# An attention, mixing and FFN kernel: weights in one lasting place per chunk, the first pairs' working memory laid where the later pairs' will be, pooled attention of a later pair ranked ahead, sums in place

## The chip, the cores and the metric

The kernel runs on one core of a Trainium2 chip. Its time is the device time in microseconds (us) of one execution. Times of one kernel differ a little from run to run: the three runs of the kernel before took 1030.01, 1033.21 and 1035.8 us. What is predicted is the median of such runs of the changed kernel.

## The reference

Two heads of a batch are handled together and are called a *pair* here: 8 batches of 8 heads make 32 pairs, four to a batch.

```
q_d, k_d, v_d = means of q, k, v over 4 neighbouring positions      # 576 -> 144
out_up    = repeat(softmax(q_d k_d^T / 8) v_d, 4)                    # pooled attention
out_local = softmax(q k^T / 8 where |i-j| < 4, else -1e9) v          # 7 neighbours
x  = (out_up + out_local), heads side by side                        # [8, 576, 512]
h  = x^T U V        (U: 576 x 32, V: 32 x 576)                       # mixing over positions
u  = x + h^T
out = u + relu(u w_ch1) w_ch2       (512 -> 2048 -> 512, the FFN)
```

## The kernel before, in words

**Precision.** TensorE works on numbers of a shorter format. So every operand of the large products is split into a high part and a low part (`W1H`/`W1L`, `uH`/`uL`, `hH`/`hL`), and one product becomes three matmuls: high by high, high by low, low by high.

**The FFN** is cut into steps (batch, t, fc): 8 batches, two halves t of 288 positions, 16 chunks fc of 128 hidden columns, 256 steps in all. `ffn1` (L889) makes one chunk of the hidden layer with 12 matmuls into a PSUM bank `ps_h`; ScalarE (ACT) writes `hH` (L897), VectorE (DVE) writes `hL` (L898); `ffn2` (L913) adds the chunk to four accumulators `acc` with 12 matmuls. Step i of `ffn2` stands about three steps behind step i of `ffn1`. The first 19 steps of `ffn1` have only one bank, `h0`, so each waits for the `hL` of the one before it; after that the banks h0 and h1 alternate.

**The weights.** Each of 16 chunks of w_ch1 and 16 of w_ch2 (512 KB each) is loaded raw and converted by `convert`: an ACT operation (L343), three DVE operations (L345, L347, L349), an ACT operation for the high part (L354) and a GpSimd (POOL) operation for the low part (L357). The DVE operations use a PSUM bank `y`: an accumulator's (`acc2`/`acc3`) for w_ch1, the bank h1 for w_ch2. The raw chunks of w_ch1, and the first three of w_ch2, share three buffers with `Pt`, a tile of the later pairs, so a load waits until a buffer comes free. The converted w_ch1 lies in two large tiles that last; the converted w_ch2 lies in `w2p`, a region that the pool `early` holds until the first batch's attention has ended. The operation called "late" hands it over. The first `ffn2` also waits for all 16 high parts of w_ch1, because their conversion uses its accumulators' banks.

**The attention** has two forms. The four pairs of batch 0 (*early pairs*) are done on the chip in one go (`early_global`, `local_blocks`, `early_mix`), with working tiles in the pool `early`. The other 28 (*late pairs*) go through memory:

- `late_global`: loads `gq` and `gT` (L580), POOL averages them (L429, L431), `late_scores` makes local and pooled scores in one bank (`ps_b`, L720 and L727), and the local scores are stored as `s_s`; then exponentials `E`, their transposes `ps_t`, the product `ps_a`, the scaled result `od` (L567), stored four-fold as `up_s` (L572).
- `local_attn`: the local scores come back as `sc`; a chain of small DVE and ACT operations (`ms` L771, `lmx`, `lsm`, `lrl`) ends in the weights `at`; `up_s` comes back as `ul`; five times, ACT copies a piece of `ul` into `Pt`, POOL multiplies seven shifted values into it (L800) and DVE sums it into `acc` (L805, an SBUF tile of this function, not the accumulator); `acc` is stored as `x_s`.
- `mix_part`: `x_s` is loaded twice, as `xL` and as `Y`; DVE transposes Y (L839), POOL makes the low part of xL (L841), TensorE (PE) makes `ps_hu` (L849) and `ps_u` (L864), and the result is split into `uH` (ACT) and `uL` (POOL, L872) for the FFN.

**The order of the work** is set when the program is built. A planner plays through all operations with estimated durations and, on each engine, takes among those that are ready the one with the smallest priority number. The pairs count 0, 10, 20 and so on (a pair's scores a little earlier, its local part +1, its mixing +2), weights have numbers of their own, the FFN's matmuls 1000 and more, so that they fill what is left. What comes out is one fixed order for each engine. On the chip each engine follows its order and waits where it must. All transfers are issued by SP, in its fixed order too.

Of the kernel before, what the change touches and what calls it, by code (L numbers as in the profile page):

```python
# [51 lines left out]
class Plan:  # L52
# [9 lines left out]
    def op(self, eng, dur, fn, r=(), w=(), prio=0.0, after=(), lat=None, move=0.0, at=0.0):  # L62
# [137 lines left out]
def attn_mix_ffn_kernel(ctx: ExitStack, tc, q, kp, vp, qT, kT, v, U, Ub, V, w1, w2, mask, band, eye, ex, pool, vw, vn, ident, outT):  # L200
# [16 lines left out]
    W1S, W2P, W2S = 2, 20, 1  # L217
# [5 lines left out]
    W1P = 20  # L223
    W2D = 4
# [68 lines left out]
    w2p = Late()  # L293
# [36 lines left out]
    dma(lambda: nc.sync.dma_start(out=mask_sb, in_=mask), [], ["mask"], 35, 32)  # L330

    def convert(raw, pp, n, hi_out, lo_out, a, wkey, name, prio, gate=(), l0=0):
        t = buf(ffn, [128, CN], I32, name, "cT:" + name, 3)
        if gate or name == "cu" and lo_out is not None:
# [17 lines left out]
        if gate:  # L352
            done.append(plan.ops[-1])
        act(n, lambda: nc.scalar.activation(hi_out(), ta(), AF.Copy), [t, *gate], own("H"), prio)  # L354
# [6 lines left out]
    def early_raw(name):  # L361
        return buf(early_pool, [128, S], I32, name, "eraw", 1)

    def raw_buf(name):
# [676 lines left out]
```

## Time and profile before

| what | value |
|---|---|
| median of three runs | 1033.21 us |
| the profiled execution | 1031.25 us, its span from the first to the last instruction 1029.4 us |
| mean granted TensorE clock | 0.983 |
| PE busy over the span | 990.8 us (96%) |
| DVE, ACT, POOL busy | 504.4, 390.2, 550.6 us |
| first FFN matmul (batch 0) | starts at 77.15 us |
| first `ffn2` matmul | starts at 91.34 us |
| first FFN matmul of batch 1 | starts at 219.88 us |

"Busy" is the time in which an engine had at least one instruction under way. Rows with `[x <-E y]` say that the engine stood idle for x us before the row, and that what ended it was engine E's work on y. "x12" is a count of like instructions. The 1.85 us by which the profiled execution is longer than its span lie around the program.

### The profile page before, as it was taken

The numbers are of one execution on the slowest core, as the hardware profiler recorded it, in microseconds if no ns is written. First come the engines' busy times: TensorE is split into PE (matmuls) and PEld (weight loads), VectorE is DVE, ScalarE is ACT, GpSimd is POOL, SyncE is SP. The second block draws the span as 40 slices with busy tenths as digits, with TensorE's granted clock in tenths as the row PEclk, the third lists the DMA queues.
The fourth block names the chain that finished last, engine by engine and source line by source line (L and its number), as shares of the span: only waits on it lengthen the run. The fifth ranks groups of instructions, "written<-read, shape, count | busy, mean of one in ns | idle before, by whom it ended". The sixth has DMA issues, their size and how long they took to land.

```text
span 1029.4 us, 26839 instructions
## 1 busy us (share of the span) xinstructions
PE 990.8 (96%) x10792; PEld 972.9 (95%) x10792; DVE 504.4 (49%) x1022; ACT 390.2 (38%) x1239; POOL 550.6 (53%) x580
## 2 busy tenths in 40 slices
PE   5888979989999999999999999999999999999998
PEld 4677979989999999999999999999999999999998
DVE  4778986544454447544454545445654424212111
ACT  3667643433334334443343442334443232111110
POOL 3545895783756656685665756457575605211010
PEclk8899999989999999999999999999999999999999
DMA  9748854573454546555544453556555231000000
GB/s 291 200 136 237 256 132 123 133 154 98 103 142 105 142 118 148 121 120 144 121 126 115 122 122 83 122 134 156 126 135 129 78 76 35 24 1 24 1 24 24
DMA packets 222452, 120.51 MB, mean 117 GB/s; under 512 B 174756, under 2 KB 198136, under 8 KB 222328
## 3 DMA queue, kind: packets, MB, share of 16 engines
q1 hardware_dynamic: 222328, 118.79, 46.0%
q8 instruction: 85, 1.39, 0.6%
q14 instruction: 39, 0.32, 0.1%
HBM read 87.89 MB, written 30.86 MB: 115 GB/s over the span
## 4 chain that ended last, share of the span: by engine, by line
PE 90%; DVE 3%; ACT 2%; DMA 2%; issue 1%; SPq 1%; POOL 0%; DVEq 0%; ACTq 0%
PE acc L913 38%; PE ps_h L889 38%; PE ps_a L563 3%; PE ps_b L720 2%; PE ps_hu L849 2%; PE ps_t L550 1%; PE ps_b L727 1%; PE ps_u L864 1%; PE ps_v L445 1%; DMA w2r<-in_W 1%; DVE ms L771 1%; DMA ul<-up_s 1%; PE ps_u L695 1%; DMA pool_sb<-in_pool 0%; PE ps_hu L675 0%
## 5 line engine op out<-in xcount | busy, mean ns | idle before, releaser
L913 PE MATMUL acc<-hH,W 128*128 128x288 f32 x2048 | 464.0, 299 | 0.1
L913 PEld LDWEIGHTS acc<-hH,W 128*128 128x128 f32 x2048 | 344.8, 188 | 1.6 <-POOL W L357 0.5
L889 PE MATMUL ps_h<-uH,W1H 128*128 128x288 f32 x1024 | 305.9, 299 | 11.1 <-DVE hL L898 11.1
L889 PE MATMUL ps_h<-uL,W1H 128*128 128x288 f32 x1024 | 304.2, 297 | 0.0
L898 DVE SCALAR_TENSOR_TENSOR hL<-ps_h,hH 128x288 fp32r<-128x288 f32 x256 | 116.7, 456 | 382.4 <-ACT hH L897 381.6
L889 PE MATMUL ps_h<-uH,W1L 128*128 128x288 f32 x1024 | 302.9, 296 | 0.0
L913 PE MATMUL acc<-hL,W 128*128 128x288 f32 x1024 | 301.9, 295 | 0.0
L800 POOL TENSOR_TENSOR Pt<-vl,at 128x896 f32<-128x896 f32 (+1 forms) x140 | 241.9, 1806 | 90.3 <-DVE acc L805 40.2
L897 ACT ACTIVATE hH<-ps_h 128x288 fp32r<-128x288 f32 x256 | 105.1, 411 | 432.1 <-PE ps_h L889 431.8
L889 PEld LDWEIGHTS ps_h<-uH,W1H 128*128 128x128 f32 x1024 | 194.3, 190 | 12.9 <-DVE hL L898 12.6
L889 PEld LDWEIGHTS ps_h<-uH,W1L 128*128 128x128 f32 x1024 | 194.7, 190 | 0.0
L889 PEld LDWEIGHTS ps_h<-uL,W1H 128*128 128x128 f32 x1024 | 194.4, 190 | 0.0
L913 PEld LDWEIGHTS acc<-hL,W 128*128 128x128 f32 x1024 | 192.7, 188 | 0.0
L805 DVE TENSOR_REDUCE acc<-Pt 128x128 f32<-128x1024 f32 (+1 forms) x140 | 151.1, 1105 | 6.7 <-ACT Pt L794 2.4
L841 POOL TENSOR_TENSOR xL<-xL,xH 116x640 fp32r<-116x640 f32 x28 | 44.0, 1572 | 96.5 <-ACT xH L840 83.5
L872 POOL TENSOR_TENSOR uL<-xT,uH 128x288 fp32r<-128x288 f32 x56 | 44.3, 816 | 84.5 <-ACT uH L870 84.4
L924 POOL TENSOR_TENSOR o<-uH,uL 128x288 f32<-128x288 f32 x64 | 49.8, 817 | 53.0 <-DMA out_t<-o 53.0
L521 POOL TENSOR_TENSOR vr<-vr 72x256 f32<-72x256 f32 x56 | 41.6, 743 | 41.7 <-DMA vr<-in_v 37.0
L745 ACT ACTIVATE se<-ps_b 96x114 f32<-96x114 f32 x112 | 40.0, 357 | 59.3 <-PE ps_b L720 37.8
L794 ACT ACTIVATE Pt<-ul 128x128 f32<-128x128 f32 (+1 forms) x140 | 50.3, 444 | 18.7 <-DVE acc L805 14.5
L536 ACT ACTIVATE E<-ps_b,nb 72x144 f32<-72x144 f32 x112 | 40.9, 372 | 0.6
L531 DVE TENSOR_REDUCE mx<-ps_b 72x2 f32<-72x288 f32 x56 | 23.4, 449 | 27.6 <-ACT se L745 27.6
(137 smaller groups left out, 986.4 us busy)
## 6 DMA issues: line engine op xcount, KB each, us to landing
vl<-in_vp SPq DMA_DIRECT2D x56, 240.0 KB
out_t<-o SPq DMA_DIRECT2D x64, 144.0 KB
w1r<-in_W SPq DMA_DIRECT2D x16, 512.0 KB
w2r<-in_W SPq DMA_DIRECT2D x16, 512.0 KB
gT<-in_kT SPq DMA_DIRECT2D x28, 291.0 KB
gq<-in_qT SPq DMA_DIRECT2D x28, 288.0 KB
vr<-in_v SPq DMA_DIRECT2D x56, 144.0 KB
up_s<-od SPq DMA_DIRECT2D x112, 72.0 KB
```

The source lines that it names most:

```text
L521: pool_tt(256, lambda x=x: nc.gpsimd.tensor_tensor(out=x()[:, :, 0:2, :], in0=x()[:, :, 0:2, :], in1=x()[:, :, 2:4, :], op=ALU.add), [x], ...
L536: act(SD, lambda a=a, hh=hh, nb=nb: nc.scalar.activation(Es[hh]()[:, a, :], pooled_view(ps[hh])[:, a], AF.Exp, bias=nb()[:, a:a + 1], scal ...
L794: act(n * D, lambda n=n, ps=ps, Pt=Pt: nc.scalar.activation(Pt()[:, :n, :, 7], ul()[:, ps, :], AF.Copy), [ul], [(Pt, 1)], prio, 0.16)
L800: nc.gpsimd.tensor_tensor(out=Pt()[:, :n, :, 0:7].rearrange("p s d o -> p o s d"), in0=win, in1=at()[:, ps, :].rearrange("p s o -> p o s") ...
L805: dve(8.5 * n * D, lambda n=n, ps=ps, Pt=Pt: nc.vector.tensor_reduce(out=acc()[:, ps, :], in_=Pt()[:, :n], axis=AX.X, op=ALU.add), [(Pt, 0 ...
L841: pool_tt(640, lambda: nc.gpsimd.tensor_tensor(out=xL(), in0=xL().bitcast(F32), in1=xH().bitcast(F32), op=ALU.subtract), [xL, xH], [xL], prio)
L872: pool_tt(TN, lambda uH=uH, uL=uL, uf=uf: nc.gpsimd.tensor_tensor(out=uL()[:, hp, :], in0=uf(), in1=uH()[:, hp, :].bitcast(F32), op=ALU.su ...
L889: nc.tensor.matmul(ps()[:, :TN], w[:, dc, fs], u()[:, dc, :], start=(n == 0), stop=(n == 3 * NDC - 1))
L897: last_h[i] = act(TN, lambda: nc.scalar.activation(hH(), ps()[:, :TN], AF.Relu), [ps], [hH], FIRST, 0.05)
L898: dve(TN, lambda: nc.vector.scalar_tensor_tensor(hL(), ps()[:, :TN], 0.0, hH().bitcast(F32), op0=ALU.max, op1=ALU.subtract), [ps, hH], [hL ...
L913: nc.tensor.matmul(ac[e]()[:, :TN], W2[fc]()[:, w, es], hx(), start=(fc == 0 and n == 0), stop=(fc == NFC - 1 and n == 2))
L924: pool_tt(TN, lambda e=e, o1=o1: nc.gpsimd.tensor_tensor(out=o1()[:, :TN], in0=uH()[:, e, :].bitcast(F32), in1=uL()[:, e, :].bitcast(F32), ...
```

## The change

**Weights.** Every chunk, of w_ch1 and of w_ch2, now has one lasting place in a pool `wts`, opened first. The raw chunk lands there and the converted one, of the same size, takes its place. A load waits for the conversion four chunks back (`WD`). The chunks come in a new sequence: the first four of w_ch1, then one of w_ch1 and one of w_ch2 in turn, with priority numbers from 30 up (before, w_ch1 had 20 to 50, and w_ch2 20 to 35 behind "late"). The first 12 chunks are converted through the accumulators' banks and the first `ffn2` waits for their high parts alone; the other 20 go through the bank h1. U's blocks and V, needed by the early pairs, land raw in places of the last w_ch2 chunks.

**Memory.** The pool `early` now lies where the late pairs' pools `loc`, `glo` and `mix` will be. These open when the first batch's attention has ended ("late"), and every operation on their tiles comes after that. The FFN no longer waits for "late".

**Ranks.** `late_global` of a pair gets the number p - 10.5 in place of p: ahead of the local part of the pair before it.

**Sums in place.** `Pt` is summed back into `ul` (two buffers now); the tile `acc` goes. `gh`, the first average, and `od` share one buffer in the late pairs. The early pairs' `ps_hu` and `ps_u` use the accumulators' banks 0 and 1.

The instructions are the same in number and kind: 8792 matmuls, 1024 DVE, 1113 ACT, 585 POOL and 884 SP instructions in both, as the order lists them.

The core of the diff:

```diff
+        deps.update(d for k in (*r, *w) for d in getattr(getattr(k[0] if isinstance(k, tuple) else k, "pool", None), "gate", ()))
...
-    W1S, W2P, W2S = 2, 20, 1
+    W1F, WS = 4, 0.4
-    W1P = 20
-    W2D = 4
+    W1P = 30
+    WD = 4
+    LEAD = 10.5
+    NA = 12
...
-        if gate or name == "cu" and lo_out is not None:
+        if own_bank:
             y = buf(ps_h, [128, CN], I32, "y_h", "h1:" + name, 1)
...
-    def raw_buf(name):
-        return buf(loc, [128, 2 * CN], I32, name, "Pt:raw", 3)
+    def raw_in(f, name):
+        return buf(wts, [128, 2 * CN], I32, name, f"W2_{f}:{name}")
...
+    W1 = [buf(wts, [128, 2, NDC, 128], F32R, f"W1_{f}", f"W1_{f}:w") for f in range(NFC)]
+    W2 = [buf(wts, [128, 2, DM], F32R, f"W2_{f}", f"W2_{f}:w") for f in range(NFC)]
+    weights, done = [], []
+
+    def load_w(w, src, hi, lo, a, prio, dprio):
+        weights.append(w)
+        raw = buf(wts, [128, 2 * CN], I32, "wr", w.tag + ":raw")
+        dma(lambda: nc.sync.dma_start(out=raw(), in_=src), [], [raw], dprio, 525,
+            after=done[len(done) - WD:len(done) - WD + 1] if len(done) >= WD else ())
+        convert(raw, 128, CN, hi, lo, a, w, "c" + w.tag[1], prio, len(done) >= NA)
...
-        gh = work(e, glo, [128, SD, 2], F32, "gh")
+        gh = work(e, glo, [128, SD, 2], F32, "gh", None if e else "god:h")
-        od = g([QH, 4, D], "od")
+        od = buf(glo, [QH, 4, D], F32, "od", "god:o", 1)
-        ph = psum(ps_m, "ps_hu", "m:x", 2)
+        ph = psum(ps_acc, "ps_hu", "acc0:x", 1)
-            pu = psum(ps_m, "ps_u", "m:x", 2)
+            pu = psum(ps_acc, "ps_u", f"acc{1 - t}:x", 1)
-        acc = lb([128, NPOS, D], "acc")
-        ul = lb([128, NPOS, D], "ul")
+        ul = lb([128, NPOS, D], "ul", bufs=2)
-                out=acc()[:, ps, :], in_=Pt()[:, :n], axis=AX.X, op=ALU.add), [(Pt, 0), (Pt, 1)], [(acc, p0)], prio)
+                out=ul()[:, ps, :], in_=Pt()[:, :n], axis=AX.X, op=ALU.add), [(Pt, 0), (Pt, 1)], [(ul, p0)], prio)
...
-        mm_op[i] = op(PE, PH, mm, ur + [f"W1_{fc}H", f"W1_{fc}L"] + ["late"] * (i >= 3), [ps], FILL + i,
+        mm_op[i] = op(PE, PH, mm, ur + [(W1[fc], "H"), (W1[fc], "L")], [ps], FILL + i,
-            first = [f"W1_{f}H" for f in range(NFC)] * (i == 0)
+            first = [(w, "H") for w in weights[:NA]] * (i == 0)
...
-                s_s = late_global(b, hp, up_s, p)
+                s_s = late_global(b, hp, up_s, p - LEAD)
...
-    for f in range(NFC):
-        load_w1(f, W1P + W1S * f)
-    plan.op(DVE, 0.0, w2p.open, [], ["late"], 27, after=early_ops, lat=0.0)
-    for f in range(NFC):
-        load_w2(f, W2P + W2S * f)
-    load_u(38)
+    for c in range(NFC + W1F):
+        if c < NFC:
+            load_w1(c, W1P + WS * (2 * c - min(c, W1F)))
+        if c >= W1F:
+            load_w2(c - W1F, W1P + WS * (2 * c + 1 - W1F))
+    late = plan.op(DVE, 0.0, open_late, [], [], 27, after=early_ops, lat=0.0)
+    for p in (loc, glo, mix):
+        p.gate.append(late)
+    load_u(36)
```

Two places show how the fixed order moves. The first is SP's order around the first late pair's loads. `gq` and `gT` are its queries and keys, `vw` and `vn` belong to the early pairs, `w1r` and `wr` are raw weight chunks. Before:

```order
L592 DMA vn<-in_vn 128x640
L401 DMA w1r<-in_W 128x1024 x2
L586 DMA vw_108<-in_vw 48x1152 x2
L330 DMA mask_sb<-in_mask 128x63
L580 DMA gq<-in_qT 128x576
L580 DMA gT<-in_kT 128x582
L393 DMA vraw<-in_V 128x576
```

and now:

```order
L383 DMA ur<-in_U 116x320
L405 DMA wr<-in_W 128x1024 x2
L585 DMA vw_99<-in_vw 48x1152 x2
L405 DMA wr<-in_W 128x1024 x7
L579 DMA gq<-in_qT 128x576
L579 DMA gT<-in_kT 128x582
L518 DMA vr<-in_v 72x2x256
L967 DMA mask<-in_mask 128x63
L708 DMA vl<-in_vp 64x960 x2
L405 DMA wr<-in_W 128x1024 x3
```

Before, six weight chunks are issued ahead of the first late pair's loads; now it is fifteen, and the sixteenth chunk is issued behind them.

The second place is DVE's order where the FFN begins. `hL` follows one `ffn1` step each, `mx<-ps_b` reads the first late pair's scores, and a row that writes `c_...` is the last of a conversion's three. Before, from the first `hL` on:

```order
L898 SCALAR_TENSOR_TENSOR hL<-ps_h,hH 128x288
L531 TENSOR_REDUCE mx<-ps_b 72x2 x2
L347 SCALAR_TENSOR_TENSOR y_a<-w1r,y_a 128x512
L349 SCALAR_TENSOR_TENSOR c_1184<-w1r,y_a 128x512
L345 TENSOR_SCALAR y_a<-c_1290 128x512
L898 SCALAR_TENSOR_TENSOR hL<-ps_h,hH 128x288
```

and now, from the second `hL` to the fourth:

```order
L896 SCALAR_TENSOR_TENSOR hL<-ps_h,hH 128x288
L347 TENSOR_SCALAR y_h<-c_1177 128x512
L349 SCALAR_TENSOR_TENSOR y_h<-wr,y_h 128x512
L351 SCALAR_TENSOR_TENSOR c_1177<-wr,y_h 128x512
L347 TENSOR_SCALAR y_h<-c_1213 128x512
L896 SCALAR_TENSOR_TENSOR hL<-ps_h,hH 128x288
L349 SCALAR_TENSOR_TENSOR y_h<-wr,y_h 128x512
L351 SCALAR_TENSOR_TENSOR c_1213<-wr,y_h 128x512
L896 SCALAR_TENSOR_TENSOR hL<-ps_h,hH 128x288
L530 TENSOR_REDUCE mx<-ps_b 72x2 x2
```

The first late pair's scores are read behind the fourth `hL` instead of the first. Ahead of the first `hL` DVE finishes 11 conversions of weight chunks instead of 14, so 21 are left for the time of the FFN's first steps instead of 18.

More of the change, by code (lines that the diff above doesn't have):

```diff
@@ L283, in attn_mix_ffn_kernel, with __init__, open_late @@
     class Late:
-        pool = None
+        def __init__(self, name):
+            self.name, self.pool, self.gate = name, None, []
         def open(self):
-            early.__exit__(None, None, None)
-            self.pool = ctx.enter_context(tc.tile_pool(name="w2p", bufs=1))
+            self.pool = ctx.enter_context(tc.tile_pool(name=self.name, bufs=1))
         def tile(self, *args, **kw):
             return self.pool.tile(*args, **kw)
-    w2p = Late()
+    loc, glo, mix = (Late(n) for n in ("loc", "glo", "mix"))
+    def open_late():
+        early.__exit__(None, None, None)
+        for p in (loc, glo, mix):
+            p.open()
     band_sb = early_pool.tile([128, NS * KL], BF16, name="band_sb")
@@ L329, in attn_mix_ffn_kernel, with convert @@
     dma(lambda: nc.sync.dma_start(out=ex_sb, in_=ex), [], ["ex"], 2.0, 147)
-    dma(lambda: nc.sync.dma_start(out=mask_sb, in_=mask), [], ["mask"], 35, 32)
-    def convert(raw, pp, n, hi_out, lo_out, a, wkey, name, prio, gate=(), l0=0):
+    def convert(raw, pp, n, hi_out, lo_out, a, wkey, name, prio, own_bank=False, l0=0):
         t = buf(ffn, [128, CN], I32, name, "cT:" + name, 3)
-        if gate or name == "cu" and lo_out is not None:
+        if own_bank:
             y = buf(ps_h, [128, CN], I32, "y_h", "h1:" + name, 1)
@@ L351, in convert @@
         own = lambda k: [wkey + k] if isinstance(wkey, str) else [(wkey, k)]
-        if gate:
+        if not isinstance(wkey, str):
             done.append(plan.ops[-1])
-        act(n, lambda: nc.scalar.activation(hi_out(), ta(), AF.Copy), [t, *gate], own("H"), prio)
+        act(n, lambda: nc.scalar.activation(hi_out(), ta(), AF.Copy), [t], own("H"), prio)
         if lo_out is None:
@@ L390, in load_v @@
         for c in range(2):
-            raw = early_raw("vraw")
+            raw = raw_in(NFC - 2 - c, "vraw")
             dma(lambda raw=raw, c=c: nc.sync.dma_start(
@@ L887, in mm @@
             for dc in range(NDC):
-                for w, u in ((W1H, uH), (W1H, uL), (W1L, uH)):
-                    nc.tensor.matmul(ps()[:, :TN], w[:, dc, fs], u()[:, dc, :],
+                for w, u in ((0, uH), (0, uL), (1, uH)):
+                    nc.tensor.matmul(ps()[:, :TN], W1[fc]()[:, w, dc, :], u()[:, dc, :],
                                      start=(n == 0), stop=(n == 3 * NDC - 1))
```

53 lines of the change are left out of this document (20 added, 33 removed).

## The prediction

> **What bounds the kernel now.** First the page, for the whole span:
>
> ```profile
> span 1029.4 us, 26839 instructions
> PE 990.8 (96%) x10792; PEld 972.9 (95%) x10792; DVE 504.4 (49%) x1022; ACT 390.2 (38%) x1239; POOL 550.6 (53%) x580
> ```
>
> PE is busy nearly all the time, and the change leaves its matmuls as they are. Only idle time, or time at a low clock, can be won. Where that lies, the busy times by stretch tell (columns: stretch, its length, busy us and instructions of PE, of its weight loads, of DVE, ACT and POOL, then granted clock, DMA share, GB/s):
>
> ```profile
> 0.00:77.00 77.00, 55.87 (x950) 47.67 (x951) 48.29 (x109) 43.23 (x130) 36.52 (x56) 0.89 0.69 210
> 77.00:160.00 83.00, 71.67 (x885) 68.45 (x884) 69.94 (x125) 51.43 (x147) 60.45 (x61) 0.94 0.73 200
> ...
> 220.00:900.00 680.00, 680.00 (x7371) 674.38 (x7371) 329.77 (x672) 253.51 (x838) 400.52 (x412) 1.00 0.48 114
> ```
>
> From 220 to 900 us PE never stops and its clock is full. Everything to be won lies before 220: the early pairs up to 77.15 (stage one), then the FFN of batch 0 with the late pairs of batch 1 beside it, up to 219.88 (stage two). The waits of PE name what ends them in stage two (total, times, longest):
>
> ```profile
> PE ps_h L889 <- DVE hL L898: 11.1, 7, 5.8
> PE ps_u L864 <- DVE stk L854: 2.7, 1, 2.7
> ```
>
> How much PE work stage two holds follows from the steady part: a group of 12 FFN matmuls takes 1.59 us (two pieces of the chain), and in 600 us stand 1933 matmuls of line 889, 1944 of line 913 and 220 of line 849, ten for each late pair (three answers, in this order):
>
> ```profile
> 168.01 1.60 PE acc L913 x12
> 169.61 1.59 PE ps_h L889 x12
> 250.00:850.00 600.00, 282.59 (x1933) 1.00 0.51 121
> 250.00:850.00 600.00, 296.56 (x1944) 1.00 0.51 121
> 250.00:850.00 600.00, 16.83 (x220) 16.48 (x220) 1.00 0.51 121
> ```
>
> (1933 + 1944) / 12 x 1.59 = 513.7, and the other 86.3 us over 22 pairs make 3.9 us a pair. Stage two has 64 groups (101.8 us) and, counting PE's pieces in the order, some 5.3 pairs' worth (20.7): 122.5 of its 142.7 us (219.88 less 77.15). So 20 us are lost there, and what they hang on is DVE and POOL, which convert weights meanwhile.
>
> **Stage one: when the FFN starts.** The last early pair's scores, and what follows them:
>
> ```profile
> 50.88 1.16 PE L458 MATMUL ps_s<-smk,smq 64*72 64x144 f32 x8
> 54.84 0.19 ACT L473 ACTIVATION_READ_ACCUMULATOR E_e<-ps_s,nb 72x1 f32 x1
> 60.42 0.41 ACT L491 ACTIVATE E_e<-ps_t 72x288 f32<-72x288 f32 x1
> 60.88 0.73 PE L498 MATMUL ps_a<-vs_e,E_e 128*72 128x64 f32 x8
> 64.12 1.04 PE L659 MATMUL ps_ba<-vw,et 38*32 38x64 f32 x80
> 71.79 1.31 PE L675 MATMUL ps_hu<-ob,Ublk 128*64 128x128 f32 x10
> 74.58 0.37 PE L692 MATMUL ps_u<-Vst,stk 128*128 128x288 f32 x1 [1.05 <-DVE stk L681]
> 77.15 0.38 PE L889 MATMUL ps_h<-uH,W1H 128*128 128x288 f32 x1
> 20.00:51.00 31.00, 24.84 (x502) 21.40 (x503) 18.02 (x44) 18.64 (x60) 14.60 (x19) 0.78 0.79 233
> ```
>
> Behind those scores stand, in PE's order before, `ps_u` of all four pairs and `ps_hu` of the last three; in the changed order `ps_u` of the first two pairs and `ps_hu` of the second and third stand ahead of them. From the rows, `ps_hu` takes 71.79 to 74.58 with its hand-over, some 1.8 of it on PE, and `ps_u` 74.58 to 77.15, 2.6. Moved ahead are two of each, 8.8 us of PE. What stays behind the scores: about 4.5 us of PE (`ps_u` of the third pair 2.6, `ps_ba` 1.0, transposes), longer than the 54.84 - 52.04 = 2.8 us to the exponentials and so in its cover; then twice transpose, copy and `ps_a` (0.41 + 0.73 and as much again with hand-overs, 3), `od`, and `ps_hu` and `ps_u` of the last pair with hand-overs (5.4): 13.5 us to the first FFN matmul, where it is 77.15 - 52.04 = 25.1 now. Were the 8.8 simply added ahead, the start would come at 52.04 + 8.8 + 13.5 = 74.3, 2.8 us earlier. But PE stood idle for 31 - 24.84 = 6.2 us between 20 and 51, at a clock of 0.78, and the moved work can fill that: at best -9. Three conversions fewer stand on DVE before the FFN. Against it, V's two raw halves now go ahead of the second pair's loads:
>
> ```profile
> vraw<-in_V SPq DMA_DIRECT2D x2, 288.0 KB
> ```
>
> At the 210 GB/s of the first stretch that is 2.7 us, if PE waits for them. Bounds 0 and -9; I take **-4**, since most of that idle time was waiting on ACT and DVE, whose queues hold only a little less.
>
> **Stage two: the conversions.** The rows of one conversion's DVE operations and of POOL's, and the busy share of both while w_ch2 is converted (one answer for DVE, one for POOL):
>
> ```profile
> L345 DVE TENSOR_SCALAR y_h<-c 128x512 int32<-128x512 int32 x16 | 11.0, 687 | 3.4 <-ACT c L343 3.2
> L347 DVE SCALAR_TENSOR_TENSOR y_h<-w2r,y_h 128x512 int32<-128x512 int32 x16 | 11.0, 689 | 0.2
> L349 DVE SCALAR_TENSOR_TENSOR c<-w2r,y_h 128x512 int32<-128x512 int32 x16 | 10.8, 677 | 0.4
> L357 POOL TENSOR_TENSOR W<-c,W 128x512 fp32r<-128x512 f32 x16 | 20.7, 1295 | 9.0 <-ACT W L354 8.6 <-PE ps_a L563 0.3
> 80.20:143.00 62.80, 53.76 (x103) 0.97 0.81 225
> 80.20:143.00 62.80, 48.42 (x47) 0.97 0.81 225
> ```
>
> Three conversions more fall into stage two: 3 x 2.05 = 6.2 us of DVE and 3.9 of POOL. DVE had 62.8 - 53.8 = 9 us free there, so they cost between 0 and 6.2; I take **+3**, since each `hL` queues behind them on DVE in order and PE waits for `hL`.
>
> **Waits that go.** Rows of PE in stage two:
>
> ```profile
> 84.69 0.40 PE L889 MATMUL ps_h<-uH,W1H 128*128 128x288 f32 x1 [2.15 <-DVE hL L898]
> 85.20 0.44 PE L889 MATMUL ps_h<-uH,W1H 128*128 128x288 f32 x1
> 85.44 0.44 PE L889 MATMUL ps_h<-uL,W1H 128*128 128x288 f32 x1
> 153.77 0.61 PE L889 MATMUL ps_h<-uH,W1H 128*128 128x288 f32 x1 [5.84 <-DVE hL L898]
> ```
>
> The first `ffn1` steps now run without `ffn2` between them, since the first `ffn2` waits for all of w_ch1 (it starts four steps in). After the 2.15 us wait the matmuls follow each other at 0.24 us, where 1.59 / 12 is 0.13: ten at the low clock cost another 1.1. In the changed order `ffn2` comes in after the second step and covers the `hL`. I count -2.15 - 0.5 (the wait before it) - 1.1, and +1.1 for the one uncovered step that stays: **-2.6** (0 to -3.7).
>
> The wait of 5.84 us is another thing. DVE had the `hL` queued behind one instruction:
>
> ```profile
> 145.37 6.28 DVE L771 SCALAR_TENSOR_TENSOR ms<-sc,mask_sb 128x63 f32<-128x63 f32 x1
> L771 DVE SCALAR_TENSOR_TENSOR ms<-sc,mask_sb x28: 209/218/6281, 93.7 to 849.4; 128x63 f32<-128x63 f32 x28
> 145.02 2.33 POOL L924 TENSOR_TENSOR o<-uH,uL 128x288 f32<-128x288 f32 x3
> 151.12 0.44 POOL L523 TENSOR_TENSOR vs<-vr 72x128 f32<-72x128 f32 x1
> ```
>
> It takes 0.218 us in the median and took 6.28 once, while POOL ran without a break from 145.02 to past 151.12. The step behind it ran at the low clock (chain of waits), 1.65 too long, so this cost 7.5 us:
>
> ```profile
> 153.77 3.24 PE ps_h L889 x12
> ```
>
>  It is a collision of two moments and both move. It can go, or come back elsewhere: 0 to -7.5; I take **-5**, as one of the 28 such instructions met it.
>
> The Trainium skill (SBUF — State Buffer, Who interferes with whom) says that a DVE instruction with two SBUF inputs waits for a GpSimd instruction that reads SBUF until that one has ended. The row agrees as to who waits, and not as to how long: seven POOL instructions passed, not one. By the page, the 2.5 us that I leave for a collision would be at most one POOL instruction, some 2 us, and the sum half a us lower.
>
> **The late pairs start later.** Their memory opens only when the early pairs have ended, and SP comes to `gq` behind fifteen weight chunks. The first scores now stand behind four `ffn1` and two `ffn2` groups, 9.5 us, where one stood ahead. A transfer of 288 KB took this long to land in that phase (chain of waits):
>
> ```profile
> 100.53 5.31 DMA ul<-up_s
> ```
>
> With some 2 us for the issue and 4 for POOL's averages (a conversion, 1.3, stands between them) the scores' operands are there 11 to 12 us after the gate, 9.5 of it under cover: PE waits between 0 and 5.3; I take **+2**. Behind it, from the fourth pair's `ps_a` on, both orders have the same way to go (24 `ffn1` steps done there in both), so the end of stage two shifts with the rest.
>
> **Nothing elsewhere.** The other ranks, the sums in place and the shared buffers act on late pairs, which PE does not wait for from 220 us on: 0 there. Without that cover each pair's local part (POOL, some 9 us) would show.
>
> **Sum**: -4 + 3 - 2.6 - 5 + 2 = -6.6. The profiled execution took 1031.25, so 1024.6; it was 2 us below the median of its runs, 1033.21, so 1026.6. I say **1026**.
>
> **Rivals.**
>
> *Stage two loses nothing but its end.* Weights are ready in the order in which the FFN wants them, and all of the 20 us goes but about 4 at the batch's border (the 2.7 us wait and the low clock). With -4 from stage one: 1033.2 - 20 = 1013. For it: no `ffn2` waits for all of w_ch1 any longer. Against it: DVE and POOL stay nearly full until the last conversion, around step 17 in both orders.
>
> *Nothing moves.* Stage one was bound by its loads (-1), the three conversions cost 5 of their 6.2 us, another wait takes the place of most of the 5.84 (-2): -1 + 5 - 2.6 - 2 + 2 = +1.4, 1034. For it: DVE's work ahead of `ffn1` step 16 is the three conversions longer, and DVE was nearly full there.
>
> *Slower: the late pairs' own pace decides.* The first late scores and the mixing of batch 1's last pair now stand at:
>
> ```profile
> 78.91 0.33 PE L727 MATMUL ps_b<-smk,smq 64*32 64x144 f32 x6
> 215.62 0.47 PE L849 MATMUL ps_hu<-xH,Ust 116*64 116x128 f32 x5
> ```
>
> 136.7 us apart. If this way is set by the pairs' own chain through DVE, POOL and memory, and not by PE's order, it starts at 9.5 + 1.1 + 2 = 12.6 us after the FFN's start instead of 1.8: +10.8, less 4 from stage one, 1040. It decides once the chain needs more than some 126 us. For it: POOL at 77% of the phase and a gate that was not there. Against it: before, the pairs ran beside the conversions from the start and stood waiting for their ranks, and the changed order has 58 FFN groups between the two points instead of 63.
>
> **Numbers.** Forecast 0.47 (own range 1020 to 1030), full recovery 0.17 (1013), nothing 0.20 (1034), slower 0.16 (1040). A difference under 0.5% cannot be told from none: that is 1028.0 to 1038.4. Faster: 0.8 of the forecast and all of the recovery, 0.55; slower: 0.14 of the last case and 0.02 of the third, 0.16; the same: 0.29. Range 1011 to 1040: it holds the forecast, nearly all of the third case and most of the others.
>
> **What would show it.** The first FFN matmul near 73 us (later than 77: stage one was wrong). The first `ffn2` within 6 us of it. PE's waits for `hL` near 5 us in place of 11.1. The first late scores with a wait of 2 us or so. Batch 1's first FFN matmul near 213. From there to the end 809.5 us, as now (1029.4 - 219.88): a longer rest would mean that a late pair comes too late, and the prediction would be wrong in what it leaves at nothing.

## The result, and the profile after

The changed kernel takes **1041.38 us** (median; 1038.88 to 1045.62), the kernel before, run beside it, 1030.9. The ratio is 1.011, with an interval of 1.007 to 1.015: it is slower, by about 1.1%, where 1026 was forecast. The profiled execution took 1045.05 us, 3.7 above its median; the one of before 1031.25. The page of after, whole span, and the chain that ended last by engine:

```profile
span 1043.3 us, 26946 instructions
PE 997.7 (96%) x10792; PEld 975.7 (94%) x10792; DVE 507.8 (49%) x1022; ACT 384.6 (37%) x1239; POOL 550.1 (53%) x580
PE 82%; DVE 7%; DMA 3%; ACT 3%; issue 2%; POOL 2%; SPq 1%; DVEq 0%; ACTq 0%; POOLq 0%
```

DVE stands on the chain with 7% where it had 3%. To see where, the program is cut by a count that every kernel here shares: there are 256 `hL`, one for each FFN step, and the first 32 are batch 0's. The windows for `hL` alone (stretch, length, busy us and count), before and then after:

```profile
0.00:223.20 223.20, 14.49 (x32) 0.93 0.68 186
223.20:1022.20 799.00, 102.20 (x224) 1.00 0.41 98
```

```profile
0.00:226.20 226.20, 14.48 (x32) 0.95 0.66 187
226.20:1036.00 809.80, 101.84 (x224) 1.00 0.40 96
69.64 0.45 DVE L896 SCALAR_TENSOR_TENSOR hL<-ps_h,hH 128x288 fp32r<-128x288 f32 x1
226.34 0.46 DVE L896 SCALAR_TENSOR_TENSOR hL<-ps_h,hH 128x288 fp32r<-128x288 f32 x1 [0.48 <-ACT hH L895]
1035.43 0.46 DVE L896 SCALAR_TENSOR_TENSOR hL<-ps_h,hH 128x288 fp32r<-128x288 f32 x1 [2.72 <-ACT hH L895]
```

The first `hL` of batch 0, the first of batch 1 and the last of all stand at 80.2, 223.3 and 1021.6 us before, and at 69.6, 226.3 and 1035.4 after. So stage one became 10.6 us shorter, stage two 13.6 longer (156.7 in place of 143.1), and the rest 10.8 longer (809.1 in place of 798.3). The rest is where nothing was expected to change. PE's three longest waits there, where there were none before (after, from 223 us on), and the one stretch that holds most of it (columns as in the prediction):

```profile
PE ps_b L726 <- DVE od L566: 3.3, 1, 3.3
PE ps_u L863 <- DVE stk L853: 2.8, 2, 1.5
PE ps_h L887 <- DVE hL L896: 1.9, 1, 1.9
380.00:400.00 20.00, 14.04 (x189) 13.08 (x188) 14.32 (x16) 5.66 (x18) 12.26 (x11) 0.95 0.45 91
```

What happened at 380 to 400, from the timelines of DVE, POOL, ACT and PE of after:

```profile
382.01 0.46 ACT L793 ACTIVATE Pt<-ul 128x128 f32<-128x128 f32 x1 [3.33 <-DMA ul<-up_s]
384.79 0.73 POOL L520 TENSOR_TENSOR vr<-vr 72x256 f32<-72x256 f32 x1 [3.10 <-DMA vr<-in_v]
385.48 1.91 POOL L799 TENSOR_TENSOR Pt<-vl,at 128x896 f32<-128x896 f32 x1
385.72 5.51 DVE L770 SCALAR_TENSOR_TENSOR ms<-sc,mask 128x63 f32<-128x63 f32 x1 [2.52 <-DMA sc<-s_s]
387.67 3.57 POOL L799 TENSOR_TENSOR Pt<-vl,at 128x896 f32<-128x896 f32 x2
391.15 0.44 DVE L896 SCALAR_TENSOR_TENSOR hL<-ps_h,hH 128x288 fp32r<-128x288 f32 x1
396.70 0.41 DVE L566 TENSOR_TENSOR od<-ps_a,ri 72x256 f32<-72x256 f32 x1
391.65 0.40 PE L887 MATMUL ps_h<-uH,W 128*128 128x288 f32 x1 [1.92 <-DVE hL L896]
397.16 0.43 PE L726 MATMUL ps_b<-smk,smq 64*32 64x144 f32 x7 [3.29 <-DVE od L566]
L770 DVE SCALAR_TENSOR_TENSOR ms<-sc,mask x28: 192/220/5510, 91.2 to 855.4; 128x63 f32<-128x63 f32 x28
```

This reads as follows. By the new rank, POOL's work for the pooled attention of the next pair (`vr`) stands ahead of this pair's products (`Pt`). This pair's `ul` was there at 382.0, but POOL stood waiting 3.1 us for the load of `vr`; the products began only at 385.48. At 385.72 the next pair's `ms` came to DVE, an instruction of 0.22 us in the median, and stood there for 5.51, until POOL's run was over: it was *held*, as this text calls it. An `hL` that PE waited for stood behind it, and behind that the sums of the products, and `od`, which the next scores on PE wait for. That was a reading; whether the rank does it, and by this way, the experiments had to tell.

### The profile page after: what moved, and what is told of

It is laid out like the page before. It is cut to its first block, busy times and chain, and to the rows that moved or that the text cites. A ratio compares the mean times of both kernels' runs of the same rounds, so it can differ in the third digit from the quotient of the medians.

```text
span 1043.3 us, 26946 instructions
## 1 busy us (share of the span) xinstructions
PE 997.7 (96%) x10792; PEld 975.7 (94%) x10792; DVE 507.8 (49%) x1022; ACT 384.6 (37%) x1239; POOL 550.1 (53%) x580
## 4 chain that ended last, share of the span: by engine, by line
PE 82%; DVE 7%; DMA 3%; ACT 3%; issue 2%; POOL 2%; SPq 1%; DVEq 0%; ACTq 0%; POOLq 0%
PE ps_h L887 35%; PE acc L911 34%; PE ps_b L719 2%; PE ps_a L562 2%; DVE ul L804 2%; DVE ms L770 2%; PE ps_hu L848 1%; PE ps_b L726 1%; PE ps_t L549 1%; DMA ul<-up_s 1%; POOL Pt L799 1%; PE ps_u L863 1%; PE ps_v L444 1%; DMA sc<-s_s 1%; PE ps_hu L674 1%
## 5 line engine op out<-in xcount | busy, mean ns | idle before, releaser
L887 PE MATMUL ps_h<-uH,W 128*128 128x288 f32 x2048 | 455.9, 298 | 11.6 <-DVE hL L896 11.6
L887 PEld LDWEIGHTS ps_h<-uH,W 128*128 128x128 f32 x2048 | 346.0, 190 | 13.4 <-DVE hL L896 13.2
L887 PE MATMUL ps_h<-uL,W 128*128 128x288 f32 x1024 | 304.1, 297 | 0.0
L799 POOL TENSOR_TENSOR Pt<-vl,at 128x896 f32<-128x896 f32 (+1 forms) x140 | 246.1, 1806 | 108.2 <-DVE at L782 56.0
L887 PEld LDWEIGHTS ps_h<-uL,W 128*128 128x128 f32 x1024 | 194.2, 190 | 0.0
L804 DVE TENSOR_REDUCE ul<-Pt 128x128 f32<-128x1024 f32 (+1 forms) x140 | 150.7, 1102 | 21.8 <-ACT Pt L793 8.2
L359 POOL TENSOR_TENSOR W<-c,W 128x512 fp32r<-128x512 f32 x32 | 41.1, 1289 | 33.4 <-ACT W L356 33.3
L522 POOL TENSOR_TENSOR vs<-vr 72x128 f32<-72x128 f32 x56 | 26.0, 463 | 27.9 <-PE ps_a L562 26.6
L925 DVE TENSOR_TENSOR o<-acc,o 128x288 f32<-128x288 f32 x64 | 26.5, 450 | 22.0 <-PE acc L911 21.7
```

The costliest lines, as they stand in the source:

```text
L359: pool_tt(1.0 * n, lambda: nc.gpsimd.tensor_tensor(out=lo_out(), in0=ta()[l0:], in1=hi_out()[l0:].bitcast(F32), op=ALU.subtract), [t, *own ...
L799: nc.gpsimd.tensor_tensor(out=Pt()[:, :n, :, 0:7].rearrange("p s d o -> p o s d"), in0=win, in1=at()[:, ps, :].rearrange("p s o -> p o s") ...
L804: dve(8.5 * n * D, lambda n=n, ps=ps, Pt=Pt: nc.vector.tensor_reduce(out=ul()[:, ps, :], in_=Pt()[:, :n], axis=AX.X, op=ALU.add), [(Pt, 0) ...
L887: nc.tensor.matmul(ps()[:, :TN], W1[fc]()[:, w, dc, :], u()[:, dc, :], start=(n == 0), stop=(n == 3 * NDC - 1))
```

## The experiments

All numbers in one table: median, ratio to the kernel before with its interval, and the three stretches by `hL` from each kernel's profile (the first `hL` at; from it to batch 1's first; from there to the last). Names with a_ are made from the changed kernel, a0_ from it with LEAD 0, b_ from the kernel before.

| kernel | median us | ratio | first hL | stage two | rest |
|---|---|---|---|---|---|
| before | 1030.9 to 1033.2 | 1 | 80.2 | 143.1 | 798.3 |
| changed | 1041.38 | 1.0109 [1.0072, 1.0147] | 69.6 | 156.7 | 809.1 |
| a_lead0 | 1031.53 | 0.9999 [0.9968, 1.0030] | 70.9 | 151.2 | 798.5 |
| b_lead | 1041.18 | 1.0092 [1.0062, 1.0121] | 90.4 | 133.1 | 808.0 |
| a_lead85 | 1035.70 | 1.0029 [1.0004, 1.0053] | 72.2 | 154.9 | 799.8 |
| a_one_input | 1044.27 | 1.0126 [1.0074, 1.0178] | 69.1 | 157.0 | 808.5 |
| b_one_input | 1032.64 | 1.0004 [0.9982, 1.0026] | 81.8 | 145.1 | 797.1 |
| a_on_act | 1023.15 | 0.9908 [0.9870, 0.9946] | 72.9 | 147.2 | 796.8 |
| b_on_act | 1030.90 | 0.9986 [0.9965, 1.0007] | 79.5 | 143.8 | 797.8 |
| a0_on_act | 1038.11 | 1.0050 [1.0025, 1.0075] | 68.7 | 158.2 | 800.0 |
| a_on_pool | 1022.60 | 0.9895 [0.9857, 0.9934] | 68.5 | 145.3 | 796.8 |
| a_on_pool_2 (the same) | 1024.77 | 0.9938 [0.9913, 0.9964] | 70.6 | 145.7 | 797.6 |
| a0_on_pool | 1028.37 | 0.9959 [0.9927, 0.9991] | 77.9 | 150.8 | 799.2 |
| b_lead_on_pool | 1025.51 | 0.9936 [0.9914, 0.9959] | 89.3 | 129.7 | 794.7 |
| b_on_pool | 1030.06 | 0.9985 [0.9959, 1.0012] | 79.9 | 138.8 | 798.5 |
| a0_noconv | 1030.47 | 0.9983 [0.9956, 1.0010] | 70.3 | 150.3 | 799.0 |
| a0_cut | 1026.64 | 0.9955 [0.9926, 0.9983] | 69.1 | 146.8 | 799.4 |
| a_pool_cut | 1030.51 | 0.9980 [0.9951, 1.0009] | 71.6 | 150.7 | 798.0 |

The profiled execution of a0_on_pool took 1037.59, 9 us more than its median; its stretches are to be read with that in mind. Every stretch is from one execution; the two of the same kernel, a_on_pool and a_on_pool_2, differ by 0.4 us in stage two and 0.8 in the rest.

### Is it the rank?

```diff
-    LEAD = 10.5
+    LEAD = 0.0
```

> Changed kernel with the old rank of the pooled attention (LEAD 0 in place of 10.5), nothing else. Theory 'rank' (the rank of the pooled attention makes late pairs late from 223 us on): the stretch from batch 1's first FFN matmul to the end falls from 820.3 to about 810 us, the time from 1041.4 to 1030-1034. Theory 'collision' (the wait at 385 to 400 us is one DVE instruction `ms` held back while POOL works without a break): the rank moves `ms` and POOL's work against each other at random; a rest of 810 to 820, and wherever a wait for hL or od of over 1.5 us stands after 223 us, an `ms` or another two-input DVE instruction several times its median stands ahead of it. Theory 'own pace' (from the gate on the four late pairs of batch 1 go at the pace of DVE and POOL beside 21 conversions): the first late scores come later than 78 us, with PE's order pushed by the weights that now rank ahead, and the stretch 67 to 223 us (155.7) stays or grows by up to 10.

```diff
-                s_s = late_global(b, hp, up_s, p)
+                s_s = late_global(b, hp, up_s, p - 10.5)
```

> The kernel before with the new rank of the pooled attention alone (p - 10.5). Theory 'rank': the rest from batch 1's first FFN matmul on grows from 809.5 to 815-820, time 1036 to 1041. Theories 'collision' and 'own pace': the rest stays at 809 to 811 unless a DVE instruction with two SBUF inputs meets POOL's work ahead of an instruction that PE waits for; the stretch up to batch 1's first FFN matmul moves by no more than 3 us, so 1028 to 1034.

It is. Without the rank, all the rest of the change makes no difference: 1031.53 us, a ratio of 0.9999, and a rest of 798.5. The rank alone, in the kernel before, makes it as slow as the whole change: 1041.18, rest 808.0. Chain and `ms` of a_lead0:

```profile
PE 90%; DMA 3%; DVE 2%; ACT 2%; POOL 1%; SPq 1%; issue 1%; DVEq 0%; ACTq 0%; POOLq 0%
L770 DVE SCALAR_TENSOR_TENSOR ms<-sc,mask x28: 183/217/3971, 95.6 to 840.7; 128x63 f32<-128x63 f32 x28
```

Of the 28 `ms` in a_lead0 one is over 3 us (3.97, at 199 us), and none after batch 1 has begun, where the longest takes 1.64. "Own pace" had the stretch up to batch 1 stay or grow; stage two is 5.5 us shorter than in the changed kernel. In b_lead three are, at 323.8, 570.8 and 766.2 us, and the slices of 20 us in which PE is idle for over 1 us after 300 are these three places. The first is the scene of 385 us once more, with the `acc` of the kernel before for `ul`, and the second has the same wait of POOL for `vr` ahead of it (POOL, DVE and PE of b_lead):

```profile
322.38 0.74 POOL L521 TENSOR_TENSOR vr<-vr 72x256 f32<-72x256 f32 x1 [4.01 <-DMA vr<-in_v]
323.07 1.98 POOL L800 TENSOR_TENSOR Pt<-vl,at 128x896 f32<-128x896 f32 x1
323.83 5.14 DVE L771 SCALAR_TENSOR_TENSOR ms<-sc,mask_sb 128x63 f32<-128x63 f32 x1
334.66 0.43 PE L727 MATMUL ps_b<-smk,smq 64*32 64x144 f32 x8 [3.89 <-DVE od L567]
569.63 0.73 POOL L521 TENSOR_TENSOR vr<-vr 72x256 f32<-72x256 f32 x1 [4.87 <-DMA vr<-in_v]
570.33 1.97 POOL L800 TENSOR_TENSOR Pt<-vl,at 128x896 f32<-128x896 f32 x1
```

In b_lead stage one also grew by 10 us and stage two shrank by as much: late pairs' work went ahead of the early pairs'. Batch 1 began at 223.5 all the same, so there the whole loss by the rank stands in the rest. In the changed kernel the rank costs 14.8 us between the profiled executions (rest 10.6, stage two 5.5, stage one -1.3) and 9.9 between the medians; that of the changed kernel lay 3.7 above its median and that of a_lead0 1.3 below.

### First try to take the collision away

```diff
-    scalar_tensor_tensor(ms, sc, 0.125, mask, mult, add)
+    tensor_scalar(ms, sc, 0.125, -2.0, mult, add)
-    tensor_tensor(sb, ms, mx broadcast, subtract)
+    tensor_scalar(sb, ms, 1.0, 0.0, mult, add)
-    tensor_tensor(at, ex, rl broadcast, mult)
+    tensor_scalar(at, ex, 0.2, 0.0, mult, add)
```

> Changed kernel in which the three DVE instructions of 128x63 with two SBUF inputs in the local part (ms, the subtraction of the row maximum, the product with 1/sum) have one input and a constant in place of the other: mask, row maximum and normalisation are left out, the number of instructions and elements is the same. Theory 'collision': no `ms` above 0.4 us, the waits at 385 to 400 us go (6 us of idle time and some 1.5 of low clock), the rest from 223 us on is 810 to 813 instead of 820.3, time 1031 to 1035 against 1041.4. Theory 'own pace' adds: the stretch 67 to 223 stays at 153 to 156 us. Theory 'rank': the rest stays at 817 to 821 and the time within 2 us of 1041.

> The same edit in the kernel before (mask, row maximum and normalisation left out, three DVE instructions with one input). Theory 'collision': the wait of 5.84 us for hL at 153.77 goes, 5 to 7.5 us with the low clock behind it: 1031 becomes 1023.5 to 1026, and the rest from batch 1 on stays at 809 to 810. If DVE was only held up by what it had to do anyhow, the time stays within 2 us of 1031.

The edit did not take away what it was meant to. Instructions with one input were held just the same (the group of `ms` in a_one_input, and the row that answers to 385.72):

```profile
L770 DVE TENSOR_SCALAR ms<-sc x28: 159/184/5534, 90.4 to 854.6; 128x63 f32<-128x63 f32 x28
384.37 5.53 DVE L770 TENSOR_SCALAR ms<-sc 128x63 f32<-128x63 f32 x1 [2.15 <-DMA sc<-s_s]
```

Times did not fall either (1044.27; 1032.64), so these two speak neither for nor against the collision as a cause. That the number of inputs is what counts is refuted for this form.

### The three operations on another engine

The same three operations on ACT (mask, row maximum in the difference and normalisation left out), with the rank, without it, and in the kernel before:

```diff
-    dve: scalar_tensor_tensor(ms, sc, 0.125, mask), tensor_tensor(sb, ms, mx), tensor_tensor(at, ex, rl)
+    act: activation(ms, sc, Copy, scale=0.125), activation(sb, ms, Copy), activation(at, ex, Copy, scale=0.2)
```

> Changed kernel (rank 10.5 kept) with the three small operations of the local part (ms, the subtraction, the product `at`) on ACT in place of DVE, 128x63 each; mask, row maximum in the difference and normalisation are left out. No DVE instruction with more than a reduction is left in that chain, so POOL's runs cannot hold it back. If the new rank costs time through DVE instructions that stand held beside POOL's products ('held'): the waits after 226 us (6 us at 380 to 400, 1.5 at 640, 1.3 at 770) go, from batch 1's first hL to the last one 799 to 802 us in place of 809.1, time 1031 to 1034. If the new rank costs time because it puts the next pair's pooled attention ahead of this pair's local part, whatever DVE is held by ('rank alone'): 806 to 810 us, time 1038 to 1042.

> The same edit in the kernel before (mask, row maximum in the difference and normalisation left out), as a control for what the move to ACT does by itself, and for the wait of 5.84 us at 153.77. From batch 1 on 798 to 799 us as before by either theory. 'PE's order sets the end of stage two' (the reading of the prediction): the wait goes and batch 1's first hL comes 5 to 7.5 us sooner, time 1024 to 1026. 'The late pairs set it': the pair's own chain only gets shorter by about what `ms` was held, if that pair was on it, so between 0 and 6 us.

> LEAD 0 and the three operations on ACT (mask, row maximum in the difference and normalisation left out): the control to the 1023.15 of the same edit with LEAD 10.5. 'Held' alone: the rank then makes no difference, 1021 to 1026. If the rank ahead is worth something by itself once nothing is held (the pooled result is there sooner for the local part in the crowded time after the FFN's start): 1027 to 1031, batch 1's first hL at 221 to 223 in place of 220.1.

With the rank the kernel falls from 1041.4 to 1023.15, the rest from 809.1 to 796.8: "held" had foretold 799 to 802 and 1031 to 1034, so the rest came out a little below what was said, and stage two gained 9.5 us besides. In the kernel before the edit makes no clear difference (1030.90, an interval of 0.997 to 1.001): no wait for `hL` in stage two is over 2.2 us now, the 5.84 behind the `ms` of 6.28, for which the prediction had -5, has gone, and batch 1 begins at 223.3 as before. a0_on_act came out against both its expectations, 1038.11: its rest is 800.0, near the others, but its stage two is 158.2, where PE waits 6.1 us for one `xH`. Nothing is held there, so the length of stage two has other reasons as well.

Now with the whole computation, on POOL (the mask enters eight times as large, and 1/8 goes into the exponential):

```diff
-    dve: scalar_tensor_tensor(ms, sc, 0.125, mask); tensor_tensor(sb, ms, mx); tensor_tensor(at, ex, rl)
+    pool: tensor_tensor(ms, sc, mask8, add); tensor_tensor(sb, ms, mx, subtract); tensor_tensor(at, ex, rl, mult)
-    act: Exp(sb)
+    act: Exp(sb, scale=0.125)
```

> Changed kernel (rank 10.5 kept) with the whole computation, and the three operations of the local part that were held (ms, the subtraction of the row maximum, the product `at`) on POOL in place of DVE; the factor 1/8 goes into the exponential. They queue behind POOL's own products (1.8 us each), but hold nothing on DVE. 'Held' (DVE instructions that stand still while POOL works are what the rank costs): from batch 1's first hL on 797 to 800 us, time 1021 to 1028. If it was rather that POOL and DVE have too much to do in the local part, three more POOL operations a pair (some 0.9 us, 25 us in all) make it no better: 1036 to 1044.

> The same with LEAD 0. 'Held': with LEAD 0 only one such instruction over 3 us was left (199 us, 3.97 us), so the gain over the 1031.5 of LEAD 0 is small: 1024 to 1031; from batch 1 on 797 to 799 us.

> The changed kernel with ms, the subtraction and `at` on POOL once more, in five rounds, to narrow its interval (four runs so far, ratio 0.9895 [0.9857, 0.9934]). 'Held': 1020 to 1025, ratio 0.988 to 0.993.

> The kernel before with the new rank (p - 10.5) and the three operations on POOL, the whole computation. 'Held': what the rank alone cost from batch 1 on (808.0 us against 798.3) goes here too: 797 to 801 us, and no PE wait over 1 us is left there. Its stage one stays long (the first hL at 90 us against 80), since early and late pairs mix there; so 1026 to 1033 in all. 'Rank alone': 806 to 810 us, 1038 to 1043.

> The kernel before, old rank, with the three operations on POOL, the whole computation: the missing corner of the square of rank and engine. If nothing is held in either case and the rank has a worth of its own (the batch's pooled results are there sooner): 1029 to 1033 here, against the 1025.5 with the new rank. If the move to POOL is what gives the whole gain and the rank is worth nothing by itself: 1024 to 1027.

"Held" holds. a_on_pool takes 1022.60, and 1024.77 in the second, longer measurement (the upper end of the 1020 to 1025 expected), with an interval of 0.991 to 0.996: it beats both kernels. a0_on_pool and b_on_pool came within the times expected with "held", b_lead_on_pool half a microsecond below. The page and the operations of a_on_pool_2:

```profile
PE 990.0 (97%) x10792; PEld 970.7 (95%) x10792; DVE 469.0 (46%) x938; ACT 385.6 (38%) x1239; POOL 573.2 (56%) x664
PE 91%; ACT 2%; POOL 2%; DVE 2%; DMA 1%; issue 1%; SPq 1%; DVEq 0%; POOLq 0%; ACTq 0%
L770 POOL TENSOR_TENSOR ms<-sc,mask x28: 311/320/378, 92.4 to 824.0; 128x63 f32<-128x63 f32 x28
```

POOL has 23 us more to do (573.2 against 550.1) and the kernel is 17 us faster; `ms` takes 0.38 us at the most. There is no PE wait left from 220 us on. And the square of rank and engine is whole in the kernel before, medians in us:

| | three operations on DVE | on POOL |
|---|---|---|
| before, old rank | 1031 to 1033 | 1030.1 |
| before, new rank | 1041.2 | 1025.5 |
| changed, LEAD 0 | 1031.5 | 1028.4 |
| changed, new rank | 1041.4 | 1024.8 |

The move alone gives little (-1 to -3; in the kernel before the interval holds 1). The rank costs 8 to 10 us with the three operations on DVE, and nothing with them on POOL. There the kernels with it are some 4 us faster (4.6 and 3.6 between the medians; by the ratios 0.5% and 0.2%, the second within the noise). So what the rank costs comes through the instructions that are held on DVE. Moving the operations also changes the planner's order, and no run separates that. But two different moves, to ACT and to POOL, both take the cost away, and the one-input form, which is still held, does not.

### A smaller rank

```diff
-    LEAD = 10.5
+    LEAD = 8.5
```

> Changed kernel with LEAD 8.5 in place of 10.5: the next pair's pooled attention (10k + 1.5) then stands behind this pair's local part (10k + 1) and ahead of its mixing alone (10k + 2). 'Rank alone' in proportion to what is passed by: between the two, 1034 to 1038, from batch 1 on 802 to 806 us. 'Held': only a rank ahead of the local part lets one pair's `ms` meet another pair's products on POOL; so 1030 to 1034 with no `ms` above 3 us after 226 us.

The rest is 799.8 and no `ms` after 226 us is above 1.4 us, as "held" has it: in the rest only a rank ahead of the local part does harm. The total, 1035.7, is above the 1030 to 1034 of "held" and within the 1034 to 1038 of "rank alone", because of stage two: 154.9, with one long wait of PE for `xH` (waits of PE in a_lead85, total, times, longest):

```profile
PE ps_hu L848 <- ACT xH L839: 10.5, 1, 10.5
```

### What sets the length of stage two

LEAD 0, and the last 20 of 32 weight chunks without their three DVE operations and without POOL's low part (the matmuls read the high part in its place):

```diff
+        if not bare:
             dve: y <- t;  y <- w(1), y;  t <- w(0), y
         act: W high <- t
-        if lo_out is None:
+        if lo_out is None or bare:
             return
         pool: W low <- t, W high
...
+        convert(..., bare=len(done) >= NA)
```

> Changed kernel with LEAD 0, and with the last 20 of the 32 weight chunks brought over only by ACT: their three DVE operations and POOL's low part are left out, and the matmuls read the high part where they would read the low one. It takes some 41 us of DVE and 26 of POOL out of the time after the FFN's start. 'The late pairs go at the pace of a crowded DVE and POOL': batch 1's first hL, 222.1 us with LEAD 0, comes at 195 to 208, time 1004 to 1018. 'The late pairs go at the pace of their own chain through memory' (latency of transfers, SP's order): 215 to 222, time 1024 to 1031.

It takes 37 us from DVE and 27 from POOL (462.6 and 524.9 us busy, against 499.9 and 551.4 in a_lead0), and batch 1 begins at 220.7 us instead of 222.1. So with LEAD 0 a crowded DVE and POOL do not set it. The stretches of a0_noconv show what does, in outline:

```profile
120.00:187.00 67.00, 67.00 (x806) 66.17 (x806) 32.14 (x73) 27.84 (x99) 44.50 (x47) 1.00 0.55 129
187.00:217.00 30.00, 10.74 (x159) 8.47 (x158) 14.31 (x27) 11.54 (x41) 20.63 (x24) 0.59 0.64 160
```

By `bare` the chunks after the first 12 are meant. PE, no longer held up by conversions, is done with batch 0's FFN at 187 us, and then is busy for 10.7 us of 30: it has nothing to do until batch 1's last pairs are ready. They set the end of stage two here, not the FFN. The whole table points the same way: the first `hL` stands anywhere between 68.5 and 90.4 us, and batch 1's first between 213.8 and 228.7 in no relation to it. But how far PE is out of work at that end differs from kernel to kernel (200 to 220 us of a_lead0, of after, of before and of b_lead):

```profile
200.00:220.00 20.00, 12.31 (x172) 10.72 (x171) 9.37 (x19) 7.78 (x28) 11.67 (x13) 0.78 0.43 106
200.00:220.00 20.00, 14.65 (x196) 13.65 (x195) 12.67 (x20) 8.26 (x30) 15.07 (x16) 0.91 0.60 148
200.00:220.00 20.00, 17.33 (x226) 16.97 (x224) 9.48 (x20) 9.41 (x33) 16.72 (x17) 0.96 0.70 149
200.00:220.00 20.00, 20.00 (x169) 19.88 (x167) 10.56 (x20) 9.11 (x32) 18.02 (x18) 1.00 0.55 121
```

PE stands idle for 7.7, 5.4, 2.7 and 0 us. So for the kernel before, and for b_lead, it is not shown that the late pairs alone set the end of stage two.

What in the pairs' way sets their pace, the last pair of runs was to tell: `ul` loaded from v, without waiting for the pooled result (which is left out of the output), once with LEAD 0 and once in a_on_pool.

```diff
-            in_=up_s ..., after the two stores of up_s
+            in_=v[b, h0:h0 + 2] ..., after nothing
```

> LEAD 0, and `ul` of the late pairs is loaded from v in place of `up_s` (same bytes and pattern): the local part no longer waits for the pooled attention of its pair, and the pooled result is left out of the output. 'The late pairs' own chain sets the end of stage two': one link through memory less (store of up_s, load of ul, some 8 to 10 us a pair), so batch 1's first hL comes at 208 to 217 instead of 222.1, time 1018 to 1027. If the end of stage two is set by how much work the engines or the transfers have to do in it: 220 to 223, time 1029 to 1033.

> The changed kernel with the three operations on POOL, and `ul` of the late pairs loaded from v in place of `up_s` (the pooled result is left out of the output). If the late pairs' own chain still sets the start of batch 1: its first hL comes 4 to 8 us sooner than 213.8, at 206 to 210, time 1014 to 1019. If nothing of it is left in the way of PE: 213 to 215, time 1021 to 1024.

They do not agree. In a0_cut (1026.64 us) batch 1 begins 6.2 us sooner (215.9), at the upper end of what the chain through memory foretold; in a_pool_cut it begins 6 us later than in a_on_pool_2 (222.3 against 216.3), and its 1030.51 us lie outside both expectations. Every edit changes what is ready when in the planner's game, and so the order of everything else. In stage two kernels in which nothing is held lie up to 12 us apart (a_on_pool_2 145.7, a0_on_pool 150.8, a0_on_act 158.2); that the order does this is my reading, and no run changes the order alone. Which link of the pairs' way counts is open.

## Why the prediction was wrong

**Stage one, -4 (0 to -9): right as to the way, too small.** The first FFN matmul stands at 67.27 in place of 77.15, -9.9, a little past the bound of -9. Between 20 and 51 us PE is now busy for 28.8 of 31 us, at a granted clock of 1.00, where it was 24.84 at 0.78. So the moved `ps_hu` and `ps_u` filled most of PE's idle time, and the clock rose; I had held the waits for ACT and DVE against it by half.

```profile
67.27 0.38 PE L887 MATMUL ps_h<-uH,W 128*128 128x288 f32 x1
```

**Stage two, the steps for conversions (+3), `hL` waits (-2.6) and the collision (-5): priced in the wrong place.** They treated PE's idle time as what there is to win. With LEAD 0 the end of the stage went its own way: taking out 20 conversions moved batch 1 by 1.4 us. What the 6.28 us `ms` of the kernel before was worth is less clear. Without it batch 1's first `hL` stands at 223.3 as before with the three operations on ACT, and at 218.7 with them on POOL, and neither time is clear of that of before. `ffn2` did come in after the second step, as said, and no gain shows for it. The collision did not go: in the changed kernel an `ms` of 5.43 us stands at 143.78, and PE waits 3.5 us for the `hL` behind it.

**The late pairs, +2: here the number of the rival was right.** "Their own pace decides" gave +10.8 for the later start of the late scores behind the FFN's start. The scores come 78.33 - 69.64 = 8.7 us after the first `hL` now, and came 1.3 us before it (78.91 and 80.19): +10.0. From the scores to batch 1's first `hL` it is 148.0 us in place of 144.4, +3.6. Together these are the 13.6 of stage two.

```profile
78.33 0.30 PE L719 MATMUL ps_b<-gT,gq 64*32 64x38 f32 x6
216.67 0.52 PE L848 MATMUL ps_hu<-xH,Ust 116*64 116x128 f32 x5 [0.87 <-ACT xH L839]
219.83 0.51 PE L848 MATMUL ps_hu<-xL,Ust 116*64 116x128 f32 x5 [2.65 <-POOL xL L840]
```

What I held against it, that the pairs had stood waiting for their ranks before, did not show: from the first late scores to the mixing of batch 1's last pair it is 138.3 us now, and was 136.7. A start of the FFN that is 10 us earlier is all but worthless here: with LEAD 0 the stretches are -9.3, +8.1 and +0.2, and the time is that of before.

**"Nothing elsewhere", 0: this is the step that made the sign wrong.** "The other ranks, the sums in place and the shared buffers act on late pairs, which PE does not wait for from 220 us on." The sums in place and the shared buffers do cost nothing there: they are all in a_lead0, whose rest is 798.5. The rank, which the step put at nothing, costs 10.6 us (809.1 against 798.5), through `ms` held on DVE with work that PE waits for queued behind it. I had the piece in hand: the 6.28 us `ms` was quoted, with its cause, and the step said that the collision "can go, or come back elsewhere", but its bounds were put at 0 to -7.5, and its place in stage two alone. Nor was it one of 28 that met POOL: nine `ms` of the kernel before took over 0.5 us, and eight of after. What the rank changed is how long the meetings are, and where. Before, one `ms` was over 3 us; after, four are (at 143.78, 199.61, 385.72 and 638.39), and PE waits for what stands behind three of them. Only at 385.72 is it the products that hold; at the other three most of POOL's run is its part of the output, as here:

```profile
638.39 3.42 DVE L770 SCALAR_TENSOR_TENSOR ms<-sc,mask 128x63 f32<-128x63 f32 x1
638.63 3.10 POOL L922 TENSOR_TENSOR o<-uH,uL 128x288 f32<-128x288 f32 x4
```

**The signs named.** The first `ffn2` came 4.6 us after the first `ffn1` (71.84), as said. The first late scores had no wait at all, in place of 2 us. PE's waits for `hL` in stage two are 9.6 us, not 5. Batch 1's first FFN matmul stands at 222.8, not near 213, and the rest told of the failure, as it was to.

The sum then was -4 + 3 - 2.6 - 5 + 2 = -6.6; by `hL` it is -10.6 + 13.6 + 10.8 = +13.8 in the profiled executions (1045.05 against 1031.25), and +10.5 between the medians. The rival "slower" had 1040 for it with a chance of 0.16, by a mechanism that gives, without the rank, a time unchanged (1031.5). That its total came near is luck: the rank's cost, which it did not have, came to it.

## What to carry to other kernels

Before you count a reordering of work off the critical path as free, look at what it puts beside what on engines of which one can hold the other up: an instruction of a fifth of a microsecond that once took 6 in the trace of before is a price waiting for a place. Where a stage ends with a hand-over (here batch 1's first pairs), ask first whether the bounding engine is out of work there; if it is, idle time earlier in the stage may not be to win (with LEAD 0 an FFN that started 9.3 us sooner gave nothing). And when one part of a change costs by a side effect, remove the side effect before you drop the part: the rank that cost 10 us cost nothing, and may be worth some 4, with three small operations on another engine.

## What the runs showed of the hardware

Three DVE instructions of 128x63 that read only SBUF were held at times while POOL worked: `ms`, the subtraction and the product `at` took up to 5.51, 0.77 and 1.59 us in the changed kernel, with medians of 0.22 to 0.23. The reductions of POOL's products, which also read SBUF, and `hL`, which has one input in PSUM, were never held there (groups of after; minimum, median, maximum in ns):

```profile
L804 DVE TENSOR_REDUCE ul<-Pt x140: 650/1208/1223, 108.6 to 869.3; 128x128 f32<-128x1024 f32 x112, 128x64 f32<-128x512 f32 x28
L896 DVE SCALAR_TENSOR_TENSOR hL<-ps_h,hH x256: 396/458/460, 69.6 to 1035.4; 128x288 fp32r<-128x288 f32 x128
```

The one-input form was held as well, for 5.53 us. The Trainium skill (SBUF — State Buffer, Who interferes with whom) has both: an instruction with two SBUF inputs contends with a GpSimd instruction that reads SBUF, `tensor_scalar` can take both ports even with one input, and `tensor_reduce` never contends. The rows agree with all three. That the wait ends with the instruction that holds the ports, they bear out in some cases only. In the kernel before, an `ms` that came during the second of three products was let through as that one ended, with the third right behind:

```profile
403.44 5.70 POOL L800 TENSOR_TENSOR Pt<-vl,at 128x896 f32<-128x896 f32 x3
406.00 1.21 DVE L771 SCALAR_TENSOR_TENSOR ms<-sc,mask_sb 128x63 f32<-128x63 f32 x1
```

But at 385.72 `ms` was let through only after three products and a `vs` had gone by back to back, and in the 6.28 us of before only after seven POOL instructions that began after it. So the cost is not bounded by one POOL instruction; what lets DVE in between two of them is open.
